# Regrouping the first loads of a gated feed-forward kernel: seven instead of ten

## The chip, the cores and the metric

The kernel runs on one core of a Trainium2 chip. The metric is the device time of one execution in microseconds (us). Medians and ranges below are over all runs; slow ones, left out of the ratios, were one run of the kernel before (166.85 us) and two of experiment 7 (168.48 and 168.56).

## The reference

With x of 2048 rows by 640, gate and up weights of 640 by 1536 and a down weight of 1536 by 640, all bf16:

```python
def reference(x, w_gate, w_up, w_down):
    g = _silu(x @ w_gate)
    u = x @ w_up
    return (g * u) @ w_down
```

## The kernel before

The rows are worked in four blocks of 512. The hidden dimension of 1536 is cut into twelve columns of 128; I call the weights of column 0 the **first slices** (gate and up, 160 KB each) and those of columns 1 and 2 the **second slices** (320 KB each). For the first block, x comes in four chunks of 128 rows and is transposed on TensorE; the other blocks are transposed by DMA later. All loads go out from two queues, SyncE's and ScalarE's:

```python
W_CHUNKS = [(0, 1), (1, 3), (3, 6), (6, 9), (9, 12)]
...
queues = (nc.sync, nc.scalar)
halves = ((0, KD // 2 + 1), (KD // 2 + 1, KD))
for c in (0, 1):
    for i, eng in enumerate(queues):
        load_x(eng, c + 2 * i, c + 2 * i + 1)
for dst, src in ((wg_sb, wg_v), (wu_sb, wu_v)):
    for eng, (k0, k1) in zip(queues, halves):
        eng.dma_start(out=dst[:, k0:k1, wslice(0, 1)], in_=src[:, k0:k1, wslice(0, 1)])
load_w(nc.sync, wg_sb, wg_v, *W_CHUNKS[1])
nc.scalar.activation(silu_first[:], ones[:, 0:1], ACT.Silu)
load_w(nc.sync, wu_sb, wu_v, *W_CHUNKS[1])
for a, b in W_CHUNKS[2:]:
    load_w(nc.sync, wg_sb, wg_v, a, b)
    load_w(nc.sync, wu_sb, wu_v, a, b)
```

So each queue carries two x chunks, then a part of the first gate slice, then a part of the first up slice; the second slices stand behind that on SyncE. TensorE's order in the first block is fixed:

```python
warm(N_WARM)                                         # 18 filler matmuls
transpose_chunk(0, [(dve, "po_a", 0, KD)])
transpose_chunk(2, [(dve, "po_b", 0, KD)])
warm(N_GAP)                                          # 4 fillers
for c in (1, 3):
    transpose_chunk(c, [(act, "po_a", 0, 2), (dve, "po_b", 2, KD)])
warm(2)
proj_pair(pg, wg_sb, fc, sb, 0)                      # first gate slice, 10 matmuls of 256 columns
proj_pair(pg, wg_sb, fc, sb, 1)
proj(pu, wu_sb, fc, sb, 0, S_BLK)                    # first up slice, 5 matmuls of 512 columns
```

After that each column needs five gate and five up matmuls, 1.08 us each group.

Of the kernel before, what the change touches and what calls it, by code (L numbers as in the profile page):

```python
# [10 lines left out]
def _body(  # L11
# [8 lines left out]
    nc = tc.nc  # L20
# [12 lines left out]
    KD = D // P  # L33
# [7 lines left out]
    W_CHUNKS = [(0, 1), (1, 3), (3, 6), (6, 9), (9, 12)]  # L41
# [10 lines left out]
    x_sb = consts.tile([P, SUB, D], bf16)  # L52
    xT = consts.tile([P, KD, S], bf16)
    wg_sb = consts.tile([P, KD, F], bf16)
    wu_sb = consts.tile([P, KD, F], bf16)
# [5 lines left out]
    x_v = x2.rearrange("(c p) d -> p c d", p=P)  # L61
    xt_v = x2.rearrange("s (kd p) -> s kd p", p=P)
    wg_v = w_gate.rearrange("(kd p) f -> p kd f", p=P)
    wu_v = w_up.rearrange("(kd p) f -> p kd f", p=P)
    wd_v = w_down.rearrange("(kf p) d -> p kf d", p=P)

    def wslice(a, b):
        return slice(a * P, b * P)

    def load_w(eng, dst, src, a, b):  # L70
        eng.dma_start(out=dst[:, :, wslice(a, b)], in_=src[:, :, wslice(a, b)])

    def load_x(eng, c0, c1):
        eng.dma_start(out=x_sb[:, c0:c1, :], in_=x_v[:, c0:c1, :])  # L74

    ones = consts.tile([P, P], bf16)
    silu_first = consts.tile([P, 1], f32)
    nc.vector.memset(ones[:], 1.0)  # L78

    queues = (nc.sync, nc.scalar)  # L80
    halves = ((0, KD // 2 + 1), (KD // 2 + 1, KD))
    for c in (0, 1):
        for i, eng in enumerate(queues):
            load_x(eng, c + 2 * i, c + 2 * i + 1)
    for dst, src in ((wg_sb, wg_v), (wu_sb, wu_v)):
        for eng, (k0, k1) in zip(queues, halves):
            eng.dma_start(out=dst[:, k0:k1, wslice(0, 1)], in_=src[:, k0:k1, wslice(0, 1)])
    load_w(nc.sync, wg_sb, wg_v, *W_CHUNKS[1])
    nc.scalar.activation(silu_first[:], ones[:, 0:1], ACT.Silu)  # L89
    load_w(nc.sync, wu_sb, wu_v, *W_CHUNKS[1])  # L90
# [66 lines left out]
    for sb in range(NSB):  # L157
        s_sl = slice(sb * S_BLK, (sb + 1) * S_BLK)
        for fc in range(KF):
# [16 lines left out]
            else:  # L176
# [5 lines left out]
                out=aT[:, fc, s_sl], in0=sg[:], in1=pu[:], op=ALU.mult  # L182
# [17 lines left out]
        for q in range(P // Q):  # L200
            nc.scalar.dma_start(
                out=out2[
                    sb * S_BLK : sb * S_BLK + n_t, DA + q * Q : DA + (q + 1) * Q
                ].rearrange("(i r) c -> r i c", r=Q),
                in_=ot_q[q * Q : (q + 1) * Q, :].rearrange("r (i c) -> r i c", c=Q),
# [106 lines left out]
def kernel(tc, *args):  # L312
    _body(tc, *args)
    tc.close()
    tc.compile()
    _trim(tc.nc)
# [30 lines left out]
```

## Time and profile before

| Kernel before | value |
|---|---|
| median of its first three runs | 163.96 us (163.82 to 164.18) |
| span in the profiled run | 162.8 us |
| TensorE busy | 159.0 us |
| first x chunk on SyncE landed / last x chunk landed | 2.41 / 4.60 us |
| first gate slice, its two parts landed | 4.85 and 5.06 us |
| first up slice, its two parts landed | 5.36 and 5.54 us |
| second gate and up slice issued | 2.80 and 3.21 us |
| second gate and up slice landed | 7.20 and 8.13 us |

A landing is the issue in the timeline plus the time to landing; the view of DMA issues has the latter rounded. For the two parts of the first up slice in the kernel before (tile, queue, KB each, us to landing):

```profile
wu_sb<-in_w_up_dram SPq DMA_DIRECT2D x1, 96.0 KB, 4.0
wu_sb<-in_w_up_dram ACTq DMA_DIRECT2D x1, 64.0 KB, 4.0
```

Issued at 1.39 and 1.52 us, they were there about 4.0 us later, before TensorE's weight load asked for them at 6.04 (the first up matmul was due at 5.05 + 1.09 = 6.14).

### The profile page before, as it was taken

The page shows a single profiled execution, that of the slowest core. Times are in us where ns is not written, and L with a number is a line of the kernel's source. Part 1 is how long each engine was busy: PE and PEld are TensorE (multiplying, and loading weights), DVE is VectorE, ACT ScalarE, POOL GpSimd, SP SyncE. Part 2 cuts the span into 40 slices and gives each one's busy share as a digit, 9 for nine tenths or more (in the row PEclk, how much of TensorE's full clock was granted, in tenths as well). Part 3 has the DMA queues.
Part 4 walks back from the last instruction along what each step waited for, and adds up shares of the span by engine and source line. Part 5 has one row for each costly group of instructions (what it writes and reads, how often), then busy time and mean ns, then how long its engine had stood idle before and what let it go on. Part 6 is the DMA issues. An engine that isn't in the chain of part 4 may idle for free.

```text
span 162.8 us, 1869 instructions
## 1 busy us (share of the span) xinstructions
PE 159.0 (98%) x766; PEld 75.3 (46%) x781; DVE 37.9 (23%) x58; ACT 42.4 (26%) x72; POOL 0.6 (0%) x6
## 2 busy tenths in 40 slices
PE   8999999999999999999999999999999999999994
PEld 7644444444444444444444444444444444445442
DVE  2322333310022333311002333331001333332000
ACT  3322222112222222221222222221213222222121
POOL 1000000000000000000000000000000000000000
PEclk9999999999999999999999999999999999999999
DMA  7999999804100000003110000000320000000302
GB/s 214 244 327 328 361 236 226 161 9 80 45 32 0 0 0 0 4 0 34 64 64 0 2 4 0 0 0 5 60 68 32 0 0 0 0 0 4 56 33 72
DMA packets 26888, 11.26 MB, mean 69 GB/s; under 512 B 17664, under 2 KB 26880, under 8 KB 26880
## 3 DMA queue, kind: packets, MB, share of 16 engines
q1 hardware_dynamic: 17968, 10.16, 22.8%
q10 hardware_dynamic: 8912, 0.98, 3.9%
q8 instruction: 6, 0.10, 0.3%
q14 instruction: 2, 0.02, 0.0%
HBM read 6.55 MB, written 2.62 MB: 56 GB/s over the span
## 4 chain that ended last, share of the span: by engine, by line
PE 96%; DMA 2%; issue 1%; SPq 0%; DVE 0%
PE pu L134 31%; PE pg L134 31%; PE po_a L213 25%; PE po_t L189 6%; DMA x_sb<-in_x_dram 2%; PE pg L149 1%; PE pt L125 0%; PE po_b L226 0%; SPq L74 0%; DVE ot_b L234 0%; PE pw L103 0%
## 5 line engine op out<-in xcount | busy, mean ns | idle before, releaser
L134 PE MATMUL pu<-xT,wu_sb 128*128 128x512 bf16 x230 | 58.9, 379 | 0.5
L134 PE MATMUL pg<-xT,wg_sb 128*128 128x512 bf16 x235 | 58.4, 379 | 0.0
L181 DVE TENSOR_TENSOR aT<-sg,pu 128x512 bf16<-128x512 f32 x48 | 33.1, 689 | 100.5 <-PE pu L134 100.5
L180 ACT ACTIVATE sg<-pg 128x512 f32<-128x512 f32 x48 | 28.7, 597 | 71.1 <-PE pg L134 70.1
L213 PE MATMUL po_a<-wd_sb,aT 128*128 128x512 bf16 x188 | 41.9, 379 | 0.2
L134 PEld LDWEIGHTS <-wu_sb 128*128 128x128 bf16 x240 | 23.5, 98 | 28.1 <-DMA wu_sb<-in_w_up_dram 0.2
L134 PEld LDWEIGHTS <-wg_sb 128*128 128x128 bf16 x235 | 22.9, 98 | 27.8 <-DMA wg_sb<-in_w_gate_dram 0.4
L213 PEld LDWEIGHTS <-aT 128*128 128x128 bf16 x192 | 18.8, 98 | 22.6
L221 ACT CAST ot<-po_a 128x512 bf16<-128x512 f32 x16 | 9.4, 585 | 32.4 <-PE po_a L213 19.3
L189 PE MATMUL po_t<-aT,wd_sb 128*128 128x512 bf16 (+1 forms) x47 | 10.3, 365 | 0.1
L189 PEld LDWEIGHTS <-wd_sb 128*128 128x128 bf16 x48 | 4.7, 98 | 5.1
L198 ACT CAST ot_t<-po_t 128x512 bf16<-128x512 f32 (+1 forms) x4 | 2.2, 558 | 11.6 <-PE po_t L189 11.6
L199 DVE STREAM_TRANSPOSE ot_q<-ot_t 128x512 bf16<-128x512 bf16 (+1 forms) x4 | 2.7, 678 | 9.0 <-ACT ot_t L198 9.0
L103 PE MATMUL pw<-ones 128*128 128x128 bf16 x24 | 2.8, 289 | 0.4 <-DVE ones L78 0.4
L234 DVE CAST ot_b<-po_b 128x128 bf16<-128x128 f32 x1 | 0.3, 291 | 9.9 <-PE po_b L226 9.9
L103 PEld LDWEIGHTS <-ones 128*128 128x128 bf16 x24 | 2.3, 136 | 0.4 <-DVE ones L78 0.4
L130 DVE COPY xT<-pt 128x640 bf16<-128x640 bf16 (+1 forms) x4 | 1.6, 424 | 3.5 <-PE pt L125 3.5
L125 PE MATMUL pt<-ident,x_sb 128*128 128x128 bf16 x20 | 1.9, 262 | 0.5 <-DMA x_sb<-in_x_dram 0.5
L125 PEld LDWEIGHTS <-x_sb 128*128 128x128 bf16 x20 | 1.5, 119 | 0.9 <-DMA x_sb<-in_x_dram 0.9
L89 ACT ACT_TABLE_LOAD x1 | 1.3, 1283 | 2.0 <-issue 2.0
L149 PE MATMUL pg<-xT,wg_sb 128*128 128x256 bf16 x10 | 1.3, 272 | 0.0
L149 PEld LDWEIGHTS <-wg_sb 128*128 128x128 bf16 x10 | 0.9, 98 | 0.1
(11 smaller groups left out, 3.5 us busy)
## 6 DMA issues: line engine op xcount, KB each, us to landing
out_dram<-ot SPq DMA_DIRECT2D x16, 128.0 KB, 1.7
wd_sb<-in_w_down_dram SPq DMA_DIRECT2D x1, 1920.0 KB, 12.0
wg_sb<-in_w_gate_dram SPq DMA_DIRECT2D x3, 480.0 KB, 7.7
wu_sb<-in_w_up_dram SPq DMA_DIRECT2D x3, 480.0 KB, 8.1
out_dram<-ot_q ACTq DMA_DIRECT2D x12, 32.0 KB, 1.9
x_sb<-in_x_dram SPq DMA_DIRECT2D x2, 160.0 KB, 3.1
x_sb<-in_x_dram ACTq DMA_DIRECT2D x2, 160.0 KB, 3.3
wg_sb<-in_w_gate_dram SPq DMA_DIRECT2D x1, 320.0 KB, 4.4
```

Of the source, the lines that this page charges most:

```text
L103: nc.tensor.matmul(pw[:, 0:P], lhsT=ones[:], rhs=ones[:], start=True, stop=True)
L125: nc.tensor.transpose(out=pt[:, kd - k0, :], in_=x_sb[:, c, kd * P : (kd + 1) * P], identity=ident[:],)
L130: copy(out=xT[:, k0:k1, c_sl], in_=pt[:])
L134: nc.tensor.matmul(ps[:, c0:c1], lhsT=w_sb[:, kd, fc * P : (fc + 1) * P], rhs=xT[:, kd, sb * S_BLK + c0 : sb * S_BLK + c1], start=(kd == 0 ...
L149: nc.tensor.matmul(pair(ps[:]), lhsT=w_sb[:, kd, fc * P : (fc + 1) * P], rhs=pair(xT[:, kd, sb * S_BLK : (sb + 1) * S_BLK]), start=(kd == ...
L180: nc.scalar.activation(sg[:], pg[:], ACT.Silu)
L181: nc.vector.tensor_tensor(out=aT[:, fc, s_sl], in0=sg[:], in1=pu[:], op=ALU.mult)
L189: nc.tensor.matmul(po_t[:], lhsT=wd_sb[:, kf, DA:D], rhs=aT[:, kf, sb * S_BLK : sb * S_BLK + n_t], start=(kf == 0), stop=(kf == KF - 1),)
L198: nc.scalar.copy(ot_t[:], po_t[:])
L199: nc.vector.transpose(out=ot_q[:], in_=ot_t[:])
L213: nc.tensor.matmul(po_a[:], lhsT=aT[:, kf, s0 : s0 + P], rhs=wd_sb[:, kf, 0:DA], start=(kf == 0), stop=(kf == KF - 1),)
L221: nc.scalar.copy(ot[:], po_a[:])
```

## The change

The intent: fewer loads at the start, so fewer issues, and no wait of the SyncE queue before the second slices. Chunks 1 and 3 become one load, the first slices go whole on ScalarE.

```diff
-    def load_x(eng, c0, c1):
-        eng.dma_start(out=x_sb[:, c0:c1, :], in_=x_v[:, c0:c1, :])
+    def load_x(eng, *chunks):
+        c_sl = slice(chunks[0], chunks[-1] + 1, 2)
+        eng.dma_start(out=x_sb[:, c_sl, :], in_=x_v[:, c_sl, :])
...
-    queues = (nc.sync, nc.scalar)
-    halves = ((0, KD // 2 + 1), (KD // 2 + 1, KD))
-    for c in (0, 1):
-        for i, eng in enumerate(queues):
-            load_x(eng, c + 2 * i, c + 2 * i + 1)
-    for dst, src in ((wg_sb, wg_v), (wu_sb, wu_v)):
-        for eng, (k0, k1) in zip(queues, halves):
-            eng.dma_start(out=dst[:, k0:k1, wslice(0, 1)], in_=src[:, k0:k1, wslice(0, 1)])
+    load_x(nc.sync, 0)
+    load_x(nc.scalar, 2)
+    load_x(nc.sync, 1, 3)
+    load_w(nc.scalar, wg_sb, wg_v, *W_CHUNKS[0])
+    load_w(nc.scalar, wu_sb, wu_v, *W_CHUNKS[0])
     load_w(nc.sync, wg_sb, wg_v, *W_CHUNKS[1])
     nc.scalar.activation(silu_first[:], ones[:, 0:1], ACT.Silu)
     load_w(nc.sync, wu_sb, wu_v, *W_CHUNKS[1])
```

## The prediction

> **What bounds the kernel now.** I read the page from the top, then the chain of waits, then the first microseconds of the timeline, then the DMA queues there. First, busy shares and the chain by engine:
>
> ```profile
> PE 159.0 (98%) x766; PEld 75.3 (46%) x781; DVE 37.9 (23%) x58; ACT 42.4 (26%) x72; POOL 0.6 (0%) x6
> ...
> PE 96%; DMA 2%; issue 1%; SPq 0%; DVE 0%
> ```
>
> TensorE is busy for 159.0 of 162.8 us and carries 96% of the chain. The diff touches no matmul, and the listing of both programs shows TensorE, VectorE and GpSimd with the same instructions in the same order. So the change can only move the moment at which the matmul stream begins, and the holes in its first microseconds. The opening of the chain (start, duration, what):
>
> ```profile
> 0.46 3.87 DMA x_sb<-in_x_dram
> 4.33 0.05 issue
> 4.37 0.73 PE pt L125 x10
> 5.10 0.11 PE pw L103 x2
> 5.21 1.09 PE pg L149 x10
> ```
>
> The load issued at 0.46 us is x chunk 1 on SyncE; it landed at 4.33. Ten transposes of chunks 1 and 3, two filler matmuls and the first gate group follow without a pause. In the timeline:
>
> ```profile
> 4.37 0.73 PE L125 MATMUL pt<-ident,x_sb 128*128 128x128 bf16 x10 [0.49 <-DMA x_sb<-in_x_dram]
> ...
> 5.05 1.25 PE L149 MATMUL pg<-xT,wg_sb 128*128 128x256 bf16 x10
> ...
> 7.25 0.76 PEld L134 LDWEIGHTS <-wg_sb 128*128 128x128 bf16 x5 [0.35 <-DMA wg_sb<-in_w_gate_dram]
> ...
> 8.17 0.92 PEld L134 LDWEIGHTS <-wu_sb 128*128 128x128 bf16 x5 [0.16 <-DMA wu_sb<-in_w_up_dram]
> ```
>
> The useful stream starts at 5.05 = 4.33 + 0.72. The weight loads at 7.25 and 8.17 wait 0.35 and 0.16 us for the second gate and up slices, but weight loads run ahead of matmuls, so I check what the matmuls lost: pg of slice 0 starts at 5.05, takes ten steps of 0.109 (start to start in the trace), then pu five of 0.216, so pg of slice 1 is due at 5.05 + 1.09 + 1.08 = 7.22. It started at 7.25. The next steps are 8.34 and 9.42, the regular 1.08 apart. The 0.35 us wait therefore cost about **0.03 us**, and the 0.16 us wait nothing.
>
> Now the loads. Before, the tenth in all and the ones near it are held at the queue:
>
> ```profile
> 1.39 0.49 SPq L87 DMA_DIRECT2D wu_sb<-in_w_up_dram  x1
> ...
> 2.80 0.37 SPq L71 DMA_DIRECT2D wg_sb<-in_w_gate_dram  x1
> 3.21 0.53 SPq L71 DMA_DIRECT2D wu_sb<-in_w_up_dram  x1
> ```
>
> The program's listing has eight DMA semaphores; the ninth load (2.80) waits for the first to come back, the tenth for the second. That is the pause from 1.88 to 2.80, which the queue's own waits show as a wait for x_sb. Bytes per window (us, ..., DMA share, GB/s), and the two queues between 3 and 4 us (packets, MB, share):
>
> ```profile
> 1.50:2.50 1.00, 1.00 (x11) 0.77 (x9) 0.00 (x0) 0.46 (x1) 0.00 (x0) 1.00 0.97 323
> 3.00:4.00 1.00, 0.88 (x11) 0.71 (x9) 0.79 (x2) 0.53 (x2) 0.00 (x0) 1.00 1.13 289
> 4.50:5.50 1.00, 1.00 (x17) 0.95 (x16) 0.64 (x2) 0.65 (x2) 0.00 (x0) 1.00 0.87 183
> ...
> q1 hardware_dynamic: 540, 0.15, 64.3%
> q10 hardware_dynamic: 336, 0.14, 49.2%
> ```
>
> Until 4.5 us the 16 DMA engines are full (about 297 GB/s from 1.5 to 4.5). Only from 4.5 to 5.5 do they run half fed, at 183 GB/s: the late second slices leave a hole. The two queues, q1 fed by SyncE and q10 by ScalarE, moved 0.15 and 0.14 MB with very different packet counts, so they share by bytes, about evenly.
>
> **What the Trainium skill says.** "DMA: Bandwidth & Descriptors", section "Issuing engines are not separate DMA queues": loads of both queues run on the same 16 engines and interleave, and a second issuer saves only issue time. This trace agrees (shares of the two queues add to 113% of 16 engines, and 297 GB/s stands while both are fed). The same page, section "Queues, rings and completion order": each engine takes its rings in turn, by packets of several descriptors, and each ring in order. The even bytes above agree; how large a turn is, no row shows plainly. "TensorE: Matmul & The Clock Gate", part "The HAM clock gate": the array starts at half clock and long idle brings that back. The trace agrees for the start (transposes 0.107 us apart at 2.5 to 3.4, 0.056 at 4.4); whether a longer pause before the second transposes would throttle it again, no run shows.
>
> **The change, part by part.**
> 1. Three fewer issues at 0.4 to 0.5 us of queue time each, and three fewer of the eight semaphores taken: seven loads go out with no wait. The second gate slice is issued at about 0.9 instead of 2.80 us, the second up slice at 1.4 instead of 3.21. What it can save on TensorE is the 0.03 us above. It also fills the hole at 4.5 to 5.5, but with bytes that are needed only at 7.2 and 8.2.
> 2. Chunks 1 and 3 become one load on SyncE, on one semaphore. Before, chunk 1 had landed at 4.33 and chunk 3 at 4.60 (issued at 0.56, landed after 4.04), and chunk 3 was met just as chunk 1's transposes (5 x 0.056) were done. Now chunk 1 cannot be transposed before chunk 3 is there. If the pair lands when chunk 3 did, the stream starts at 4.60 + 0.72 = 5.32, **0.27 us later**.
> 3. When does the pair land? The SyncE queue must move 164 + 328 = 492 KB by then instead of 328 KB, while ScalarE's queue carries chunk 2 and then both first slices. (a) Turns of whole loads: chunk 0, chunk 2, the pair, then weights, as before: 4.4 to 4.6. (b) Even bytes: SyncE's 0.49 MB beside about 0.41 MB of ScalarE's (it starts about 0.08 MB later), 0.90 MB in all. Before, the windows give 0.09 MB to 1.5 us, 0.41 to 2.5, 0.56 to 3, 0.85 to 4, so 0.90 at about 4.2; chunks were seen to land 0.3 to 0.6 us after their last packets, so 4.6 to 4.8. I take **4.65**: stream at 5.37, **+0.32**.
> 4. Both first slices, 164 KB each, ride on ScalarE alone. Before they landed whole at 5.06 and 5.54 (issued 1.03 and 1.52, 4.02 after each). The first pu matmul is now due at 5.37 + 1.09 = 6.46. Under (b) the up slice lands at 5.1 to 5.6, in time. Under (a) the second gate slice (328 KB, 1.0 us at 320 GB/s) is served between the two first slices: 5.54 + 1.0 = 6.5, just about when it is due, or 0.1 us late. I count **+0.05**.
> 5. Later loads: those of slices 3 on were early before (issued at 4.62, landed 10.45, needed at 11.58) and come no later. No cost, no gain.
>
> Sum: +0.32 + 0.05 - 0.03 = **+0.34 us**, on 163.96: **164.3 us**.
>
> **Rivals.**
> - *The early second slices help*: if holes in the first 9 us were the cost, the change would win the 0.51 us of the two waits: 163.45. For it: the waits are in the trace. Against: the regular 1.08 us steps of the matmuls across both.
> - *One load of 320 KB lands sooner than two*: with ScalarE's small packets behind only chunk 2, the pair could have most of the engines and land at 4.1 to 4.3; the stream would start 0 to 0.2 us earlier, 163.7 to 163.9. For it: fewer issues and completions. Against: engines are already full until 4.5, and even bytes give SyncE only half.
> - *The first up slice becomes the wait*: early second slices on SyncE take the bandwidth from it after the pair. If a turn favours them, both (0.66 MB, 2 us at 320 GB/s) pass it and it lands at 7.0 to 7.5: +0.6 to +1.0, 164.9. For it: ScalarE's queue now holds 1280 packets of 256 B. Against: the even bytes.
> - *The clock falls back*: the pause on TensorE before the second transposes grows from 0.49 to about 0.8 us. If it throttled, the ten transposes would cost 0.5 us more and a part of the matmuls twice: up to 166. Against: the pause is short beside 3 us of work around it.
>
> **Range and chances.** The sum of holes, and the earliest time of any load, let the time move by under 1% either way, so 2% is far off: same 0.98. Three runs of before spread over 0.36 us, as large as my shift. The first two rivals set the low end, 163.8, the third the high end, 164.9.
>
> **What would show it.** Right: the second gate and up slices issued before 2 us; one x landing at 4.5 to 4.8 that releases ten transposes in a row; the first gate matmul at about 5.4; no hole from 4.5 to 5.5 in the DMA share; the regular 1.08 us steps from then on, and everything later the same. Wrong: the first gate matmul at or before 5.05 (step 3), a wait of pu for the first up slice longer than 0.2 us (step 4), a gap after 7 us that is closed and moves the end by more than 0.1 us (step 1), or 0.107 us steps after 4 us (the clock).

## The result, and the profile after

The changed kernel took **165.59 us** (median of 6 runs, 165.24 to 166.07) beside 164.07 us (163.82 to 164.56) of the kernel before: ratio 1.0089, 95% interval 1.0065 to 1.0113. A ratio is the mean time of one kernel's runs over that of the other's in the same rounds, so it is not quite the ratio of the medians. Executions over 1.5% slower than the fastest of the same kernel are left out of the means. A second set of rounds on another occasion gave 165.32 beside 164.53, ratio 1.0054 (1.0030 to 1.0077). It is slower by 0.5 to 0.9%, within the 2% band but outside the range that was predicted.

The page of the changed kernel, busy shares and chain by engine:

```profile
PE 160.9 (98%) x781; PEld 76.0 (46%) x781; DVE 37.9 (23%) x58; ACT 42.5 (26%) x72; POOL 0.6 (0%) x6
...
PE 94%; DMA 4%; ACTq 1%; DVE 0%; issue 0%
```

DMA has doubled its share of the chain. (The 15 matmuls more are records missing from the first trace, not work; the difference in busy time is not to be read.) The chain's opening, changed kernel (start, duration, what):

```profile
1.04 6.51 DMA wu_sb<-in_w_up_dram
7.54 0.05 issue
7.59 1.25 PE pu L132 x5
8.84 1.08 PE pg L132 x5
```

The load on the chain is no longer an x chunk but the **first up slice**, issued by ScalarE at 1.04 us and landed at 7.54, after 6.51 us instead of about 4.0. The regular 1.08 us groups start only behind it. The timeline of the changed kernel around it:

```profile
0.91 0.47 SPq L71 DMA_DIRECT2D wg_sb<-in_w_gate_dram  x1
1.04 0.55 ACTq L71 DMA_DIRECT2D wu_sb<-in_w_up_dram  x1
1.43 0.53 SPq L71 DMA_DIRECT2D wu_sb<-in_w_up_dram  x1
...
4.06 1.25 PE L123 MATMUL pt<-ident,x_sb 128*128 128x128 bf16 x10
...
5.47 1.06 PEld L147 LDWEIGHTS <-wg_sb 128*128 128x128 bf16 x10 [0.22 <-DMA wg_sb<-in_w_gate_dram]
...
7.59 1.25 PE L132 MATMUL pu<-xT,wu_sb 128*128 128x512 bf16 x5 [0.78 <-DMA wu_sb<-in_w_up_dram]
```

Where the time went, from these starts: the first gate matmul came at 5.47 instead of 5.05 (+0.42), and the first up matmul, due 10 x 0.109 = 1.09 us later at 6.56, came at 7.59 (+1.03, of which some 0.08 are gate matmuls that still ran at half clock). Together 1.45 us; the spans differ by 164.2 - 162.8 = 1.4. From 7.59 on both kernels keep the same step, so nothing else matters.

Why was the load so late? The two queues of the changed kernel, first from 3 to 4 us, then (second pair) from 4 to 4.75 us; q1 is SyncE's, q10 ScalarE's (packets, MB, share of the 16 engines):

```profile
q10 hardware_dynamic: 610, 0.15, 67.9%
q1 hardware_dynamic: 176, 0.14, 41.3%
```

```profile
q1 hardware_dynamic: 376, 0.19, 87.7%
q10 hardware_dynamic: 74, 0.02, 10.7%
```

From 3 to 4 us the queues move equal bytes: the x pair on SyncE, the first gate slice on ScalarE. From 4 to 4.75 SyncE gets about ten times ScalarE's bytes, and five times its packets: the second gate slice runs, while the first up slice, issued 0.13 us after it and needed 1.1 us before it, stands. The landings are in this order: first gate 5.43, second gate 6.56, first up 7.54, second up 7.82. The engines are as busy as could be wished (window, durations, DMA share, GB/s of the changed kernel):

```profile
4.50:5.50 1.00, 1.00 (x11) 0.78 (x10) 0.52 (x2) 0.73 (x2) 0.00 (x0) 1.00 1.06 286
```

The hole of 183 GB/s was filled, as foreseen, with bytes that came too soon.

### The profile page after: what moved, and what is told of

Same layout as the page of the kernel before. It is cut to its first block, busy times and chain, and to the rows that moved or that the text cites. A ratio compares the mean times of both kernels' runs of the same rounds, so it can differ in the third digit from the quotient of the medians.

```text
span 164.2 us, 1881 instructions
## 1 busy us (share of the span) xinstructions
PE 160.9 (98%) x781; PEld 76.0 (46%) x781; DVE 37.9 (23%) x58; ACT 42.5 (26%) x72; POOL 0.6 (0%) x6
## 4 chain that ended last, share of the span: by engine, by line
PE 94%; DMA 4%; ACTq 1%; DVE 0%; issue 0%
PE pu L132 32%; PE pg L132 31%; PE po_a L211 25%; PE po_t L187 6%; DMA wu_sb<-in_w_up_dram 4%; PE po_b L224 0%; ACTq L71 0%; ACTq L75 0%; DVE ot_b L232 0%
## 5 line engine op out<-in xcount | busy, mean ns | idle before, releaser
L132 PE MATMUL pu<-xT,wu_sb 128*128 128x512 bf16 x240 | 59.6, 379 | 0.8 <-DMA wu_sb<-in_w_up_dram 0.8
L132 PEld LDWEIGHTS <-wg_sb 128*128 128x128 bf16 x235 | 23.0, 98 | 27.7
L123 PE MATMUL pt<-ident,x_sb 128*128 128x128 bf16 x20 | 2.5, 311 | 0.0
L123 PEld LDWEIGHTS <-x_sb 128*128 128x128 bf16 x20 | 2.0, 143 | 0.4 <-DMA x_sb<-in_x_dram 0.3
L128 ACT COPY xT<-pt 128x256 bf16<-128x256 bf16 x2 | 0.7, 372 | 1.5 <-PE pt L123 1.5
```

What stands on the lines that cost most here:

```text
L123: nc.tensor.transpose(out=pt[:, kd - k0, :], in_=x_sb[:, c, kd * P : (kd + 1) * P], identity=ident[:],)
L128: copy(out=xT[:, k0:k1, c_sl], in_=pt[:])
L132: nc.tensor.matmul(ps[:, c0:c1], lhsT=w_sb[:, kd, fc * P : (fc + 1) * P], rhs=xT[:, kd, sb * S_BLK + c0 : sb * S_BLK + c1], start=(kd == 0 ...
```

## The experiments

**Theory A**: the second slices, queued early on SyncE, pass the first up slice, which waits alone on ScalarE's queue. In all runs here the loads of one queue landed in the order of their issue, so the loss would be one of order. **Rival B**: the new loads are slow by themselves (the x pair on one queue, or whole slices of 256-byte packets). Later, within A: **A1**, the engines take turns of about a whole load; **A2**, they share by bytes. A further rival was not set up beforehand: that what counts is the **order of issue** over both queues, whichever queue a load is on. Experiments 4 and 8 come back to it.

All kernels gave correct results. Each was run with 5 rounds beside the kernel before.

| Experiment | median us (range) | before beside it | ratio (95%) | first up slice landed |
|---|---|---|---|---|
| change, first set | 165.59 (165.24 to 166.07) | 164.07 | 1.0089 (1.0065 to 1.0113) | 7.54 |
| change again | 165.32 (164.98 to 165.88) | 164.53 | 1.0054 (1.0030 to 1.0077) | 6.98 |
| 1 up slice on SyncE | 164.76 (163.92 to 166.3) | 164.27 | 1.0013 (0.9992 to 1.0035) | 5.90 |
| 2 x pair alone | 164.76 (164.49 to 165.04) | 164.27 | 1.0027 (1.0012 to 1.0043) | 5.62 |
| 3 whole slices alone | 167.87 (166.16 to 168.41) | 164.27 | 1.0207 (1.0173 to 1.0242) | 8.68 |
| 4 second slices held for chunk 0 | 164.67 (164.16 to 165.11) | 164.53 | 1.0006 (0.9982 to 1.0030) | 5.66 |
| 5 second slices held for the pair | 164.95 (164.67 to 166.54) | 164.27 | 1.0063 (1.0029 to 1.0098) | 5.29 |
| 6 second slices narrower | 164.73 (164.58 to 166.58) | 164.48 | 1.0047 (1.0007 to 1.0087) | 6.67 |
| 7 second slices wider | 166.22 (165.67 to 168.56) | 164.48 | 1.0103 (1.0080 to 1.0127) | 8.14 |
| 8 loads in order of need | 165.31 (164.69 to 165.62) | 164.48 | 1.0055 (1.0032 to 1.0078) | 7.49 |
| 9 as 1, pause filled | 164.35 (163.82 to 165.22) | 164.48 | 1.0011 (0.9982 to 1.0039) | 6.00 |
| 10 both first slices on SyncE | 164.62 (164.01 to 165.14) | 164.53 | 1.0003 (0.9977 to 1.0028) | 5.90 |

Landings are from each one's single profiled run. Medians of the kernel before drift by half a microsecond between sets, so ratios are what to compare.

### 1. The first up slice on the other queue

```diff
-    load_w(nc.scalar, wu_sb, wu_v, *W_CHUNKS[0])
+    load_w(nc.sync, wu_sb, wu_v, *W_CHUNKS[0])
```

> The changed kernel with one word changed: the first up slice goes out on SyncE, behind the x pair and ahead of the second slices. Theory A (the second gate and up slices, queued on the other queue, pass the first up slice): on one queue they cannot pass it, so it lands at 5.1 to 5.7 us instead of 7.54, TensorE's wait for it falls from 1.06 to under 0.2 us, and the time is 163.8 to 164.4. Rival B (the x pair on one queue, or whole 160 KB slices of 256-byte packets, are slow by themselves): the slice still lands after 6.5 and the time stays over 165.

The slice landed at 5.90 instead of 7.54, a little later than expected, and TensorE no longer waited for it. The ratio fell from 1.0089 to 1.0013, not told apart from 1. The same bytes in the same packets, put behind the x pair and ahead of the second slices, are not slow: A holds, B falls for the slices. Two things changed together, though: the first up slice changed its queue, and it was now issued before the second gate slice (0.91 and 1.43) instead of after it (1.04 and 0.91). The median of 164.76 is above what I expected, and one run took 166.3 (the plain means of all runs, 164.82 and 164.30, would give 1.0032); experiment 9 takes that up.

### 2. The x pair alone

Against the kernel before:

```diff
-    for c in (0, 1):
-        for i, eng in enumerate(queues):
-            load_x(eng, c + 2 * i, c + 2 * i + 1)
+    load_x(nc.sync, 0)
+    load_x(nc.scalar, 2)
+    load_x(nc.sync, 1, 3)
```

> The kernel before with the x pair alone: chunks 1 and 3 as one load on SyncE, the first slices still as halves on both queues. Theory A: the pair is innocent (it landed at 4.01 in the changed kernel, before chunk 3 did in the kernel before), the halves stand ahead of the second slices in both queues' order on SyncE; the first up slice lands by 6.0 and the time is 163.8 to 164.4. Rival B (the pair costs): 164.6 to 165.6, with the first gate matmul at 5.5 or later.

The slice parts landed at 5.39 and 5.62, as A had it, although the second gate slice was issued at 1.95, earlier than before. With a part of each first slice ahead of it on its own queue, that early issue did no harm. But the time, 164.76, and the first gate matmul, at 5.54, lie where rival B had them: the pair by itself costs something. The ratio, 1.0027, is a third to a half of the change's. In the profiled run the pair's landing is not the reason: at 4.24 it was earlier than those of chunk 1 (4.33) and chunk 3 (4.60) in the kernel before. What was slow there is the work behind it:

```profile
4.28 1.25 PE L126 MATMUL pt<-ident,x_sb 128*128 128x128 bf16 x10 [0.17 <-DMA x_sb<-in_x_dram]
```

The ten transposes ran at half clock, that is 0.107 us from start to start instead of 0.056, and took 1.25 us instead of 0.73. Whether the pair brings the late clock about is not shown, with one profile of each kernel. Experiments 4 and 10 hold the pair too, with the same 1.25 to 1.27 us, and their ratios are not told apart from 1; but their intervals reach 1.0030 and 1.0028, so they don't exclude a loss of this size.

### 3. The whole slices alone

Against the kernel before:

```diff
-    for dst, src in ((wg_sb, wg_v), (wu_sb, wu_v)):
-        for eng, (k0, k1) in zip(queues, halves):
-            eng.dma_start(out=dst[:, k0:k1, wslice(0, 1)], in_=src[:, k0:k1, wslice(0, 1)])
+    load_w(nc.scalar, wg_sb, wg_v, *W_CHUNKS[0])
+    load_w(nc.scalar, wu_sb, wu_v, *W_CHUNKS[0])
```

> The kernel before with four single x chunks on two queues, but both first slices whole on ScalarE, so that eight loads go out without a wait. Theory A: this part alone carries the loss; the first up slice lands at 7.0 to 7.8, TensorE waits about 1 us for it, time 165.2 to 166.0. Rival B (the loss needs the x pair on SyncE): 163.8 to 164.4.

The direction was right, the size was not: 167.87 us, over twice the loss of the change. With only two single chunks ahead of them on SyncE, the second slices now pass **both** first slices: second gate landed at 5.68, first gate 7.11, second up 8.51, first up 8.68. In the changed kernel the first gate slice was still served first; there the second gate slice stood behind the x pair, and it was also issued later than the first gate slice (0.91 and 0.56; here 0.91 and 1.05). Which of the two counted is not separated. And the long pause brought the clock down. First TensorE in the timeline, then the window after it (the number before the DMA share is the granted clock), both of this experiment:

```profile
7.15 2.31 PE L148 MATMUL pg<-xT,wg_sb 128*128 128x256 bf16 x10 [2.42 <-DMA wg_sb<-in_w_gate_dram]
```

```profile
7.10:10.40 3.30, 3.03 (x12) 1.94 (x14) 0.00 (x0) 0.60 (x1) 0.00 (x0) 0.50 1.11 323
```

After 2.4 us without work the clock was 0.50 for the next 3.3 us, and ten gate matmuls took 2.31 us instead of the 1.25 of the kernel before. Of the six runs, the five with a mean clock of 0.99 took 167.79 to 168.41 us, the one with 1.00 took 166.16.

### 4. Only the early issue undone

Against the changed kernel; SyncE's order is pinned as TensorE's is:

```diff
+    nc.gpsimd.tensor_copy(out=wg_sb[:, 0, P : P + 1], in_=x_sb[:, 0, 0:1])
     load_w(nc.sync, wg_sb, wg_v, *W_CHUNKS[1])
...
                 keep_order(mybir.EngineType.PE)
+                keep_order(mybir.EngineType.SP)
```

> The changed kernel with only the early issue undone: a one-column copy on GpSimd into the second gate slice waits for x chunk 0, so SyncE issues the second slices at about 2.7 us, as in the kernel before (2.80). Both first slices stay on ScalarE. If the early issue alone carries the loss (theory D): the first up slice lands by 5.8 and the time is 163.8 to 164.6. If the separate queue carries it (theory A1: what counts is that packets of the second gate slice are there when an engine has finished the first gate slice, at 3.8 to 4.2, and packets appear about 1.2 us after the issue): part or all of the loss stays, the slice lands at 6.3 to 7.5, time 164.8 to 165.6.

This is the experiment that settles that the early issue carries the loss. The x pair, the whole slices and ScalarE's queue are those of the change; only SyncE's issues from the second gate slice on move back, that of the second gate slice from 0.91 to about where the kernel before had it (2.80):

```profile
2.88 0.38 SPq L71 DMA_DIRECT2D wg_sb<-in_w_gate_dram  x1
```

The first up slice landed at 5.66, its weight load shows no wait, and the ratio is 1.0006:

```profile
7.00 0.85 PEld L133 LDWEIGHTS <-wu_sb 128*128 128x128 bf16 x5
```

My own bet, that part of the loss would stay, was wrong; the first-named view (D, the early issue alone) was right. The proof is in the runs, a mean of 164.68 us beside 165.39 of the change again in the same set. The one profiled run of each doesn't show it: at 165.06 us this one was the second slowest of its six, its span of 163.7 is that of the change again, because here the pair landed only at 4.52 and TensorE ran at half clock until about 6.2.

The two queues from 4 to 4.75 us, in this experiment, beside the second pair of lines shown of the changed kernel:

```profile
q10 hardware_dynamic: 495, 0.12, 74.0%
q1 hardware_dynamic: 102, 0.05, 40.2%
```

Now ScalarE's queue has the larger share: the first up slice follows the first gate slice at once, because the second gate slice is not there yet. Put together with experiments 1, 2 and 10: in these runs early issue did harm only when the slice needed first stood on the **other** queue, and the other queue did harm only with the early issue. The rival named above fits these runs as well: in experiments 1, 2, 4, 5, 9 and 10 the first up slice was issued before the second gate slice, in the change and in experiments 3, 6 and 7 after it, and it was late in just these. No experiment kept the loads and queues of the change and swapped these two issues. Experiment 8 comes nearest, and speaks against the order of issue as the whole answer.

### 5. The second slices held still longer

As experiment 4, with the copy waiting for the pair:

```diff
-    nc.gpsimd.tensor_copy(out=wg_sb[:, 0, P : P + 1], in_=x_sb[:, 0, 0:1])
+    nc.gpsimd.tensor_copy(out=wg_sb[:, 0, P : P + 1], in_=x_sb[:, 1, 0:1])
```

> The changed kernel with the second slices held: a one-column copy on GpSimd into the second gate slice waits for the x pair, so SyncE issues the second slices only at about 4.2 us. All else as in the changed kernel, both first slices on ScalarE. Theory A: nothing is queued that could pass the first up slice; it lands at 5.1 to 5.7. The second gate slice then lands at 7.0 to 7.5, about when it is due, so 163.9 to 164.7. Rival B (256-byte packets of 320 KB on one queue are slow by themselves): the first up slice lands after 6.5 even alone, time over 165.

The first up slice came at 5.29, the earliest of all, and again was no cause of waiting. But the second slices, issued at 4.55, landed at 7.70 and 8.75 and were now late themselves; the second gate group began at 7.83. In the profiled run, of 164.67 us, that group began 0.58 us later than in the kernel before: 0.40 was already there at the first gate matmul (5.46), and about 0.2 was the wait for the second gate slice. So this run exchanged one wait for another. The ratio of 1.0063 is higher because of two runs of 166.18 and 166.54, which were not profiled.

### 6 and 7. The dose

Against the changed kernel, once narrower and once wider second slices:

```diff
-    W_CHUNKS = [(0, 1), (1, 3), (3, 6), (6, 9), (9, 12)]
+    W_CHUNKS = [(0, 1), (1, 2), (2, 5), (5, 8), (8, 12)]     # experiment 6
+    W_CHUNKS = [(0, 1), (1, 4), (4, 7), (7, 10), (10, 12)]   # experiment 7
```

> The changed kernel with its second slices half as wide (weight columns of one slice, 160 KB each, instead of two; the later cuts move by one). Theory A1 (the engines take the two queues' loads in turns of a whole load, so the first up slice waits for one whole second gate slice): its turn is 160 KB shorter, so the first up slice lands about 0.5 to 0.7 us earlier, 6.8 to 7.1 instead of 7.54, and the time falls to 164.8 to 165.3. Rival A2 (the queues share by bytes, as the prediction argued from the windows; SyncE's queue is full anyway): the slice lands at 7.4 to 7.7 as before, time 165.4 to 165.8.

> The changed kernel with its second slices half again as wide (480 KB each instead of 320). Theory A1 (turns of a whole load): the first up slice lands 0.4 to 1.0 us later, 8.0 to 8.5 us, and the time rises to 166.0 to 166.8. Rival A2 (shares by bytes): it lands at 7.4 to 7.7 and the time stays 165.4 to 165.8.

TensorE's weight loads for the first up slice, in the narrow and then in the wide variant (the bracket is the idle time before it and what ended it):

```profile
6.71 0.76 PEld L132 LDWEIGHTS <-wu_sb 128*128 128x128 bf16 x5 [0.81 <-DMA wu_sb<-in_w_up_dram]
```

```profile
8.19 0.76 PEld L132 LDWEIGHTS <-wu_sb 128*128 128x128 bf16 x5 [1.94 <-DMA wu_sb<-in_w_up_dram]
```

With second slices of 160, 320 and 480 KB the first up slice landed at 6.67, 7.54 (6.98 in the second profile) and 8.14 us, and the ratio rose from 1.0047 over 1.0054 to 1.0089 to 1.0103. SyncE's queue is full in all three, so sharing by bytes (A2) would leave the landing where it was. It moved with the size of the load that goes first, as A1 has it. Turns of single packets, one from each queue, would let it move too; but in the window from 4 to 4.75 above SyncE's queue had 376 packets and ScalarE's 74. Each landing is from one profile, and the change alone spreads from 6.98 to 7.54; the intervals of the ratios overlap, so that the dose is seen in the landings and not proven in the time. The narrow variant's interval is wide because of one run of 166.58, and its median, 164.73, beat my expectation slightly. The two runs left out of the wide variant as slow, 168.48 and 168.56, have a mean clock of 0.99, as five of the six in experiment 3; they may be the same fall of the clock after a long wait (1.66 us on TensorE's matmuls here), and so part of the loss. They were not profiled.

### 8. Loads in the order of need, alternating queues

Against the kernel before:

```diff
-    for dst, src in ((wg_sb, wg_v), (wu_sb, wu_v)):
-        ...
+    load_w(nc.sync, wg_sb, wg_v, *W_CHUNKS[0])
+    load_w(nc.scalar, wu_sb, wu_v, *W_CHUNKS[0])
     load_w(nc.sync, wg_sb, wg_v, *W_CHUNKS[1])
+    load_w(nc.scalar, wu_sb, wu_v, *W_CHUNKS[1])
     nc.scalar.activation(silu_first[:], ones[:, 0:1], ACT.Silu)
-    load_w(nc.sync, wu_sb, wu_v, *W_CHUNKS[1])
```

> A candidate: the kernel before's four x chunks on two queues, then in turn the first gate slice on SyncE, the first up slice on ScalarE, the second gate slice on SyncE, the second up slice on ScalarE: eight loads without a wait, and turns of whole loads then follow the order of need. Theory A1: x lands by 4.0 to 4.6, the first gate slice by 5.1, the first up slice by 5.7, the second gate slice by 6.8; no wait on TensorE after its first gate matmul; 163.6 to 164.4. Rival A2: the same landings within 0.3 us, so this run does not tell A1 from A2; it tells both from the view that weights queued before 2 us are harmful as such, which has it over 165.

This failed, and it limits A1. If turns of whole loads were strict, the first up slice would have its turn before the second gate slice. It was also issued before it (1.04 and 1.38), so order of issue alone would have it in time as well. It landed at 7.49:

```profile
7.53 0.76 PEld L133 LDWEIGHTS <-wu_sb 128*128 128x128 bf16 x5 [0.65 <-DMA wu_sb<-in_w_up_dram]
```

In the trace, the completions of twelve of its sixteen engines had come by 5.91 us and the other four came from 6.66 to 7.49. It fits that on these four the other queue got ahead, but the trace doesn't say which engine a packet ran on, and why on four stays open. Neither A1 nor order of issue is the whole rule: order across two queues can't be relied on, and a load is complete only with its last engine. The time, 165.31, lies where the third view had it, that weights queued before 2 us are harmful as such; but experiments 1 and 10, with second gate slices issued at 1.43 and 1.99, were not told apart from the kernel before.

### 9. As experiment 1, with TensorE's pause filled

```diff
-    N_WARM, N_GAP = 18, 4
+    N_WARM, N_GAP = 18, 10
```

Theory C is that TensorE's pause before the second transposes makes full clock come late in some executions.

> The first experiment (up slice on SyncE), with ten instead of four filler matmuls in TensorE's pause before the second transposes. In its profile the first gate matmuls ran at half clock (0.213 us apart) until 8.6 us, and its runs spread from 163.92 to 166.3. Theory C[...]: with the pause filled the spread shrinks to under 0.9 us, no run is above 165.2, and the profile shows full clock at the first gate matmul or within 0.5 us of it. Rival (the spread is in the landings): as wide as before. In both the first up slice lands at 5.1 to 6.0.

The profiled run of experiment 1 was its slowest, 166.3 us, and shows why it is no verdict on the order of loads: the ten first gate matmuls ran at half clock.

```profile
5.98 2.34 PE L147 MATMUL pg<-xT,wg_sb 128*128 128x256 bf16 x10
```

With the pause filled, full clock came at 6.3 us, 0.4 after the first gate matmul, as theory C had it; but the spread of 1.4 us (2.4 in experiment 1) is above the 0.9 that I had asked for, and the highest run, 165.22, just above 165.2. Six runs of each don't settle it, and the profile speaks against the theory: with the pause filled, full clock came no sooner than in the two profiles of the change, where the pause was open (about 5.6 and 6.2 us). That the pause delays the clock is not shown.

### 10. Both first slices on SyncE

```diff
-    load_w(nc.scalar, wg_sb, wg_v, *W_CHUNKS[0])
-    load_w(nc.scalar, wu_sb, wu_v, *W_CHUNKS[0])
+    load_w(nc.sync, wg_sb, wg_v, *W_CHUNKS[0])
+    load_w(nc.sync, wu_sb, wu_v, *W_CHUNKS[0])
```

> The changed kernel with both first slices on SyncE too, behind the x pair and ahead of the second slices; ScalarE loads only x chunk 2. Theory A1: one queue is served in order, nothing can pass; first gate slice lands by 5.1, first up slice by 5.9, second gate slice by 7.2, no wait of TensorE over 0.2 us after its first gate matmul, 163.8 to 164.7. Rival (a single queue feeds the engines too slowly, so that two are needed): the landings come 0.5 us or more later and the time is over 165.

The first gate slice landed at 5.25, a little late, the first up slice at 5.90, the second gate slice at 7.00; ratio 1.0003. One queue, with second slices issued as early as 1.99 us, loses nothing. Early weights behind the urgent ones in the same queue did no harm here, and one queue fed the engines well enough. It is no gain either: no variant was shown to beat the kernel before.

### The change again

> The changed kernel unaltered, on this chip beside the two others, for a second profile: the first up slice lands at 7.2 to 7.8 us again, second in need but after the second gate slice; the time is 165.3 to 166.0 whether full clock comes early or late, because TensorE waits until 7.5 in either case.

The slice landed at 6.98, just under the expected range, again after the second gate slice (6.74), and the time was as expected. Here the first gate matmuls ran at half clock until about 6.2 us, so the slice cost less extra wait:

```profile
5.31 1.69 PE L147 MATMUL pg<-xT,wg_sb 128*128 128x256 bf16 x10
...
7.25 1.03 PE L132 MATMUL pu<-xT,wu_sb 128*128 128x512 bf16 x4 [0.25 <-DMA wu_sb<-in_w_up_dram]
```

The record of the first up matmul is missing; one step of 0.216 us earlier, it came at 7.03 instead of 6.14. Of these 0.89 us, 0.26 lie before the first gate matmul, 0.44 in the slow gate matmuls and 0.19 in the wait for the slice. In this run the late clock hid most of the late load; that may be one reason why the loss is 0.5% in one set and 0.9% in another, though the two profiles alone don't prove the share.

## Why the prediction was wrong

**The bound and the place** were right: all of the difference lies before 7.6 us, the steps of 1.08 us from then on are unchanged, and the holes that the early second slices were to close were worth almost nothing.

**Part 1** (no wait at the queue): second slices at 0.91 and 1.43 us, as said, and the hole at 4.5 to 5.5 filled, 286 GB/s instead of 183. The prediction even noted that these bytes were needed only at 7.2 and 8.2. It didn't ask what they would stand in front of. The wait at 2.80 that the change removed was doing work: experiment 4 put it back and the loss was gone. (One reading of that wait slipped, without consequence: the ninth load, at 2.80, followed the landing of chunk 2 at 2.78, not that of the first load at 2.41.)

**Parts 2 and 3** (the pair lands at 4.65): it landed at 4.01 in both profiles of the change. In the first profile the first gate matmul came at 5.47 where 5.37 was predicted, but by another road: it was held by the first gate slice, landed at 5.43, not by x. (Fifteen of the slice's sixteen engines were done by 4.68; the last one set the landing.) In the second it came at 5.31, behind transposes at half clock. Nearly the right number, for the wrong reason: luck.

**Part 4** is the step that failed: "Under (b) the up slice lands at 5.1 to 5.6, in time" and "I count **+0.05**". The slice landed at 7.54 and 6.98; measured against the matmul that waited, the term was +1.03 in the first profile and, with most of the lateness hidden by the clock, 0.19 in the second. Case (a), turns of whole loads, was short too: it had 6.5, with one second slice in between. Behind the choice of (b) is the reading that the queues "share by bytes, about evenly". That came from one window of 1 us, averaged over 16 engines, in which both queues carried loads of like size. A mean over many engines can be even while each engine serves one load at a time. The windows of the changed kernel (even from 3 to 4, about ten to one from 4 to 4.75) rule out even bytes and, with the dose of experiments 6 and 7, speak for turns of about a load, within the limits of experiment 8. (Nor did the even bytes bear out turns by packets, as the prediction had it: in its window the queues moved 540 and 336 packets.)

**The third rival** came nearest: the first up slice as the wait, landing at 7.0 to 7.5 us, 164.9 us. It had both second slices pass; by the landings only the second gate slice did (6.56 and 6.74; the second up slice came at 7.82 and 8.05). The evidence held against it, the even bytes, was the misread one, so it became the high end of the range instead of its middle. Its sum was short as well: "+0.6 to +1.0" counts from 6.46, when the slice is due in the changed kernel, and so leaves out the +0.32 of the parts before. From 6.14, where the kernel before starts its first up matmul, 7.0 to 7.5 is +0.9 to +1.4, or 164.8 to 165.3.

**Part 5** (later loads) held: nothing waits after the first up slice.

**The clock**: the ten transposes did run at half clock in the changed kernel (1.25 us against 0.73), which the prediction had as a rival with a chance of up to 166. In the first profile it is not the cause of the loss: the first up matmul waited for its slice until 7.54, and the gate group before it was through by 6.8. In the second it is the larger part of that run's delay. That it sets the change apart is unlikely: the profiled runs of experiments 1, 4, 9 and 10 had their second transposes at half clock too, and the ratios of these are not told apart from 1. What share it has in the 0.5 to 0.9% stays open. (The granted-clock column reads 1.00 in its windows all the same, because this trace holds no clock record; the steps between the matmuls, 0.107 us or 0.056, are what tells.)

## What to carry to other kernels

Before taking a wait away from a DMA queue, ask which later load it holds back, and what stands on the other queue: here an early issue gained nothing, and it cost time where a load needed sooner stood on the other queue. Put loads that are needed one after the other into one queue in that order, or give each queue its part of the urgent load ahead of the rest, as the kernel before does. Don't infer how two queues share from an even average; change the size of one load and see whether the other moves.

## What the Trainium skill lacked or had wrong

- "DMA: Bandwidth & Descriptors", section "Queues, rings and completion order", says that an engine takes queues in turn by packets of several descriptors. It lacks what follows for two queues: a load can wait for about a whole load of the other queue. Here the first up slice landed at 6.67, 7.54 (6.98 in a second profile) and 8.14 us behind second gate slices of 160, 320 and 480 KB. Nor does it say how far apart the engines of one load can finish: in experiment 8 four of sixteen finished the first up slice at 6.66 to 7.49 us, the other twelve by 5.91.
- The same page's section "Issuing engines are not separate DMA queues" says that a second issuing engine only saves issue time. The runs agree that it adds no bandwidth (one queue for the weights: ratio 1.0003), but it lacks the cost: spread over two queues, the order of need can be lost (1.0054 and 1.0089).
- "TensorE: Matmul & The Clock Gate", part "The HAM clock gate", has full clock about 4 us into sustained work, give or take 0.5. In this kernel, which has short pauses, it came at about 3.4 us in the profile before, at 5.6 and 6.2 in the two of the change, at 6.3 in experiment 9 with one pause filled and at 8.6 in experiment 1, with the first matmul at 0.4 each time. And where the table of states there asks for an idle window of about 3.4 us, a pause of 2.4 us was enough for a clock of 0.50 over the next 3.3 us (experiment 3).
